# Two late units take their whole first stage in the seven-product form, and the hand-written plans of units 4 to 8 are reordered

## The chip, the core and the metric

The kernel runs on one core of one Trainium2 chip. The metric is the device time of one execution, in microseconds (us). TensorE (PE in the profile; its weight loads are PEld), VectorE (DVE), ScalarE (ACT), GpSimd (POOL) and SyncE (SP, which issues DMAs) each work through a queue of their own, in order, and wait for each other by semaphores.

## The reference

Pooled attention is followed by an MLP mixer over tokens and channels. Eight batches, eight heads, 576 tokens, head width 64:

```
k_p, v_p = mean of 8 neighbouring tokens of k, v          # 72 keys
attn     = softmax(q @ k_p.T / sqrt(64));  x = attn @ v_p # x: 576 x 512 per batch, heads side by side
h  = relu(x.T @ w_tok1) @ w_tok2                           # 576 -> 256 -> 576, over tokens
u  = x + h.T
out = u + relu(u @ w_ch1) @ w_ch2                          # 512 -> 1536 -> 512, over channels
```

All in float32 at the interface; the kernel works in bf16 with float32 sums.

## The kernel before, in words

The channel MLP is the bulk of the work, and it is cut into nine *units* of 512 rows: units 0 to 7 are 512 tokens of batches 0 to 7, and unit 8 gathers the 64 left-over tokens of all eight. A unit has two stages. The first makes `GT = relu(w_ch1.T @ uT)`, 12 tiles of 128 channels by 512 rows (each tile is four matmuls of 512 columns, `l1_tiles`, L561, and an ACT relu, L564). The second multiplies GT by `w_ch2` and adds u.

From unit 2 on the second stage (`unit_fast`) is done in a form of Strassen's that needs seven block products instead of eight; its `product` (L777) is 12 matmuls of 256 columns. It needs four sums of blocks of GT (`g_sums`, written `=1` to `=4` in the plans, VectorE, L614 and L625, kept in the tile `area`) and adds its results with `plus` (L799).

From unit 3 on a part of the first stage has the same form (`first_fast`). The 12 tiles fall into three groups g: tiles 2g, 2g+1, 6+2g, 7+2g. `GROUPS` says which groups of a unit are done by seven products of four 256-column matmuls (L695); the others are plain tiles. One such group takes three ACT copies of sums (L733, L739, L747), three VectorE joins (`joined`, L704) with relus (L707), and one ACT relu (L723). It needs

- sums of the weights, made once per group: `in_weight_sum(i, g)`, written `%ig` in the plans; i below 4 is a VectorE operation (L664), 4 to 6 an ACT copy (L660);
- sums of blocks of uT, made per unit: `token_sum`, written `^ib` (VectorE, L614).

The last two of the seven products of a group are called `seventh` and `fourth`. Both add to the buffer of px: seventh accumulates, a VectorE join reads it, fourth accumulates on, and an ACT relu reads it. For all but the last group they are issued during the next group. For the last group they stand between the plain tiles that come last.

The rest of the work (attention, token MLP) belongs to the batch one or two ahead and is woven into the units. A unit is a generator that yields after every few matmuls, and `PLANS[n]` is a list written out by hand: at yield number i, the named steps are issued. A bare name is a step of batch n+1, `>` of n+2, `<` of n. Names that matter here: `V0 V1 K0 K1` pool v and k (POOL, L277); `kpT` PE transposes of pooled k (L283, L285); `Q0 Q1` transposes of q (DVE, L345); `s0 s1 s2` scores and exponentials (PE L357, ACT L362); `av0..av4` attention times v (PE L391, DVE L395 and L396); `at0 at1` the token MLP's first half (PE L453, ACT L446); `u0..u4` its second half (PE L468, DVE L470); `r0..r3` transposes of u to uT by PE with an ACT copy (L480, L481), `t4` the same for the tails. For batches 6 and 7 uT goes over DRAM instead: `M0 M2` write u out (`mem`, SP, L488), `M` loads it back (`v`, SP, L494) and `T0..T3` finish it (DVE, L499). `+k2c`, `+v3c` issue POOL DMAs that add the next rows of k or v to those already in (L145); POOL waits in its queue for the DMA before.

A plan sets the order on each engine's queue, not a time. Matmul results lie in two pools: `ps_one` with four buffers, taken in turn, and `ps_two` with two buffers of twice the size. A product that takes a buffer waits until what read it last is done.

Of the kernel before, what the change touches and what calls it, by code (L numbers as in the profile page):

```python
# [14 lines left out]
SUMMED = 4  # L15
BOUNCED = 6
FAST = 2
GROUPS = {3: (1,), 4: (1,), 5: (1,), 6: (1,), 7: (1, 2), 8: (1, 2)}
EARLY = 3
POOLE = mybir.EngineType.Pool  # L20
DVE = mybir.EngineType.DVE
# [36 lines left out]
}  # L58


# [1 line left out]
def kernel(  # L62
# [14 lines left out]
    nc = tc.nc  # L77
    B, H, S, D = q.shape
    P = 128
# [29 lines left out]
    w_ch2 = singles.tile([P, NM, DM], BF16)  # L109
    GT = singles.tile([P, NM, 4 * P], BF16)  # L110
# [494 lines left out]
    NH = NM // 2  # L605
    fast = {}
    lo, hi = slice(0, 256), slice(256, 512)
# [71 lines left out]
    def first_fast(n, u):  # L679
        x, U = u["uT"], token_sums(n)  # L680
        gs = GROUPS[n]
        if len(gs) == 1:
            C = [keep(name) for name in ("s1", "s5", "s4")]
            C.insert(1, C[1])
        else:
            if "C" not in fast:
                slots = att.tile([P, H * S + BP], BF16, name="ex")[:, 0:4096].bitcast(FP32).rearrange(
                    "p (i c n) -> p i c n", i=4, c=2)
                fast["C"] = [slots[:, i] for i in range(4)]
            C = fast["C"]  # L690

        def product(ps, w, mv, start=True, stop=True):
            for i in range(2):
                for k in range(2):
                    nc.tensor.matmul(out=ps[:, i], lhsT=w(i, k), rhs=mv(k), start=start and (i, k) == (0, 0),  # L695
                                     stop=stop and k == 1, skip_group_check=True)

        def bank(name):
            if name == "x":
                return ps_two.tile([P, 2, 512], FP32, name="p2")[:, 0].rearrange("p (i n) -> p i n", i=2)  # L700
            return ps_one.tile([P, 2, 256], FP32, name="p1")

        def joined(ps, other, dst):
            nc.vector.tensor_tensor(out=dst, in0=ps, in1=other, op=ALU.add)  # L704

        def relu(part):
            nc.vector.tensor_scalar_max(out=part, in0=part, scalar1=0.0)  # L707

        def summed(i, g):
            if i < 4 or (i, g) in fast.get("at", {}):  # L710
                return lambda r, k: in_sums(i, g)[:, k, r]
            m, k0 = ((2 * g, 0), (2 * g, 2), (NH + 2 * g, 2))[i - 4]
            return lambda r, k: w_ch1[(m + r) // 4][:, k0 + k, (m + r) % 4:512:4]

        def seventh(g, ps):
            sec = pairs_of(g)[1]
            product(ps, summed(2, g), lambda k: U[:, 2, k], start=False)
            joined(ps, C[1 + g % 2], GT[:, sec, hi])
            relu(GT[:, sec, hi])

        def fourth(g, ps):
            product(ps, summed(6, g), lambda k: U[:, 3, k], start=False)
            nc.scalar.activation(out=GT[:, pairs_of(g)[1], lo], in_=ps, func=AF.Relu)  # L723

        plain = [2 * g + r for g in range(3) if g not in gs for r in range(2)]
        for m in plain:
            yield from l1_tiles(u, [m])
        before = None
        for g in gs:
            f, sec = pairs_of(g)  # L730
            px, pz, py = bank("x"), bank("z"), bank("y")
            product(px, summed(4, g), lambda k: x[:, k, lo])
            nc.scalar.copy(out=C[0], in_=px)  # L733
            yield
            if before is not None:
                seventh(g - 1, before)
                yield
            product(pz, summed(0, g), lambda k: U[:, 0, k])
            nc.scalar.copy(out=C[1 + g % 2], in_=pz)  # L739
            yield  # L740
            product(py, summed(5, g), lambda k: x[:, 2 + k, lo])
            joined(py, C[0], GT[:, f, lo])
            if g == gs[-1]:
                relu(GT[:, f, lo])
            yield
            product(px, summed(1, g), lambda k: U[:, 1, k], start=False)
            nc.scalar.copy(out=C[3], in_=px)  # L747
            yield
            product(pz, summed(3, g), lambda k: x[:, 2 + k, hi], start=False)
            joined(pz, C[3], GT[:, f, hi])  # L750
            relu(GT[:, f, hi] if g == gs[-1] else GT[:, f])
            yield
            if before is not None:
                fourth(g - 1, before)
                yield
            before = px
        g = gs[-1]
        tiles = (step for m in plain for step in l1_tiles(u, [NH + m]))
        for i, _ in enumerate(tiles):
            yield  # L760
            if i == 0:
                seventh(g, before)
                yield
            elif i == 2:
                fourth(g, before)
                yield
        if not plain:
            return lambda: seventh(g, before), lambda: fourth(g, before)

    def unit_fast(n, u):  # L770
        last = n == B
        late_steps = yield from (first_fast if n in GROUPS else first_stage)(n, u)

        def product(ps, a, w, start, after, split=False):
            for i in range(2):
                for m in range(NH):
                    nc.tensor.matmul(out=ps[i] if split else ps[:, i], lhsT=a(m)[:, i * P:(i + 1) * P], rhs=w(m),  # L777
                                     start=start and m == 0 and (i == 0 or split), stop=(m == NH - 1),
                                     skip_group_check=True)
                    if (i * NH + m) % 4 == 3 and (i, m) != (1, NH - 1):  # L780
                        yield
                if split:
                    after(i)
            if not split:
                after(slice(0, 2))
            yield

        def bank(split=False):
            if split:
                return [ps_two.tile([P, 2, 512], FP32, name="p2")[:, 0, 0:256] for _ in range(2)]  # L790
            return ps_one.tile([P, 2, 256], FP32, name="p1")

        def plus(out, ps, other, then=None):
            def go(i):
                src, dst = ps[i] if type(ps) is list else ps[:, i], out[:, i]
                if len(other.shape) == 4:
                    src, dst = (x.rearrange("p (a r) -> p a r", a=4) if type(i) is int else
                                x.rearrange("p c (a r) -> p c a r", a=4) for x in (src, dst))
                nc.vector.tensor_tensor(out=dst, in0=src, in1=other[:, i], op=ALU.add)  # L799
                if then is not None:  # L800
                    then(i)
            return go
# [22 lines left out]
        s1 = keep("s1")  # L825
        for i, _ in enumerate(product(x, lambda m: GT[:, m, lo], lambda m: w_ch2[:, m, lo], True,
                                      plus(s1, x, u1lo), last)):
            yield
            if late_steps and i < 2:
                late_steps[i]()  # L830
                yield
        yield from product(y, lambda m: GT[:, NH + m, lo], lambda m: w_ch2[:, NH + m, lo], True, plus(oa[:, :, lo], y, s1))
        z = bank()
        s5 = keep("s5")
        yield from product(z, lambda m: SG[:, 0, m], lambda m: TW[:, 0, m], True, plus(s5, z, u2hi))
# [132 lines left out]
```

## Time and profile before

| | |
|---|---|
| median of 3 runs | 271.18 us (270.85 to 271.25) |
| the profiled execution | 271.6 us |
| its span, first to last instruction | 269.8 us |
| granted TensorE clock | 1.00 |
| first matmul of units 4, 5, 6, 7, 8 | 145.97, 174.84, 205.15, 226.44, 245.42 us |

The first unit begins after the early loads; units overlap with the attention of the batches ahead until unit 6, and units 7 and 8 stand nearly alone. In the timeline, one row can be several equal instructions (x20); the length of such a row runs from the first's start to the last's end. In rows of matmuls the end is modelled, so the price of one is taken from the distance between starts. Some matmul records are missing.

### The profile page before, as it was taken

How to read it: one execution, taken by the hardware profiler on the slowest of the kernel's cores; microseconds unless marked ns; L12 is line 12 of the kernel's file. 1: busy time of each engine (PE TensorE's matmuls, PEld its weight loads, DVE VectorE, ACT ScalarE, POOL GpSimd, SP SyncE). 2: the span in 40 equal slices, each digit the busy share in tenths (PEclk: the TensorE clock that was granted, in tenths of full speed). 3: DMA queues.
4: the chain of work that ended last, by engine and by line, in shares of the span. 5: the costliest groups of instructions: out<-in, count | busy, mean ns of one | idle time of the engine just before them, and what ended most of it. 6: DMA issues, size and time to landing. Idle time of an engine off the chain costs nothing.

```text
span 269.8 us, 5432 instructions
## 1 busy us (share of the span) xinstructions
PE 259.5 (96%) x2173; PEld 171.7 (64%) x2200; DVE 206.8 (77%) x427; ACT 122.7 (45%) x207; POOL 113.4 (42%) x114
## 2 busy tenths in 40 slices
PE   8999999999999999999999999999999999999992
PEld 2776454545544645776587657864785688787781
DVE  4755573751798859996978798899799889997981
ACT  1375773047444353736563637264922632613600
POOL 5847749999995428636657242420000000000000
PEclk9999999999999999999999999999999999999999
DMA  7999999959969898998995997361506510404106
GB/s 184 190 194 205 204 212 204 180 126 190 153 132 140 154 159 118 146 169 168 155 141 83 156 213 87 39 164 40 119 0 147 149 18 21 137 2 116 41 2 157
DMA packets 42081, 35.17 MB, mean 130 GB/s; under 512 B 12040, under 2 KB 34408, under 8 KB 42056
## 3 DMA queue, kind: packets, MB, share of 16 engines
q0 software_dynamic: 30672, 22.11, 55.3%
q1 hardware_dynamic: 11056, 12.39, 17.2%
q10 hardware_dynamic: 328, 0.33, 0.5%
q8 instruction: 17, 0.28, 0.4%
q14 instruction: 8, 0.07, 0.1%
HBM read 36.90 MB, written 10.49 MB: 176 GB/s over the span
## 4 chain that ended last, share of the span: by engine, by line
PE 90%; DVE 5%; ACT 2%; issue 1%; DVEq 0%
PE p L777 24%; PE p L561 22%; PE p L695 9%; PE p L592 8%; PE p L453 6%; PE p L468 5%; PE p L357 4%; PE p L391 3%; PE p L862 3%; PE p L480 2%; PE p L323 1%; DVE area L614 1%; DVE u L470 1%; ACT ex L379 1%; ACT x L426 1%
## 5 line engine op out<-in xcount | busy, mean ns | idle before, releaser
L564 ACT ACTIVATE GT<-p 128x512 bf16<-128x512 f32 x76 | 44.5, 596 | 57.6 <-PE p L561 43.7
L561 PE MATMUL p<-uT,w_ch 128*128 128x512 bf16 x274 | 69.3, 380 | 0.9 <-issue 0.4
L561 PEld LDWEIGHTS <-w_ch 128*128 128x128 bf16 x304 | 32.4, 114 | 24.1 <-issue 1.7
L362 ACT ACTIVATE ex<-p 72x1024 bf16<-72x1024 f32 (+1 forms) x42 | 31.6, 804 | 27.5 <-PE p L357 27.3
L777 PEld LDWEIGHTS <-area 128*128 128x128 bf16 x336 | 31.9, 98 | 5.3 <-issue 1.3
L777 PE MATMUL p<-area,area 128*128 128x256 bf16 x252 | 30.8, 273 | 0.0
L145 POOL DMA_DIRECT2D kr<-in_k_dram x16 | 23.4, 1495 | 15.6 <-DMA kr<-in_k_dram 15.6
L145 POOL DMA_DIRECT2D vr<-in_v_dram x16 | 23.1, 1478 | 14.2 <-DMA vr<-in_v_dram 14.2
L470 DVE TENSOR_TENSOR u<-p,x 128x512 bf16<-128x512 f32 x32 | 21.1, 680 | 8.2 <-PE p L468 8.2
L777 PEld LDWEIGHTS <-GT 128*128 128x128 bf16 x252 | 24.2, 98 | 4.9 <-issue 0.6
L592 PE MATMUL p<-w_ch,GT 128*128 128x512 bf16 x92 | 23.6, 379 | 0.2
L777 PE MATMUL p<-w_ch,GT 128*128 128x256 bf16 x168 | 20.6, 273 | 0.1
L799 DVE TENSOR_TENSOR o<-p,s 128x512 f32<-128x512 f32 (+1 forms) x28 | 17.9, 662 | 3.2 <-PE p L777 3.1
L396 DVE TENSOR_TENSOR x<-p,den 128x512 bf16<-128x512 f32 x28 | 19.4, 691 | 1.0
L468 PE MATMUL p<-AT,w_tok 128*128 128x512 bf16 x62 | 17.3, 379 | 0.5 <-DVE u L470 0.5
L799 DVE TENSOR_TENSOR s<-p,u 128x512 f32<-128x512 f32 x24 | 16.2, 680 | 2.0 <-PE p L777 2.0
L395 DVE RECIPROCAL den<-p 128x8 f32<-128x8 f32 (+1 forms) x35 | 7.0, 201 | 11.3 <-PE p L391 10.9
L391 PEld LDWEIGHTS <-ex 72*128 72x128 bf16 x280 | 12.6, 98 | 3.9 <-DVE x L396 0.2
L592 PEld LDWEIGHTS <-GT 128*128 128x128 bf16 x96 | 8.8, 98 | 9.4 <-issue 0.4
L453 PE MATMUL p<-x,w_tok 128*128 128x512 bf16 x53 | 13.7, 379 | 0.2
L446 ACT ACTIVATE AT<-p 128x512 bf16<-128x512 f32 x14 | 8.4, 597 | 12.1 <-PE p L453 11.7
L391 PE MATMUL p<-vp,ex 72*128 72x65 bf16 x280 | 13.7, 194 | 0.0
(151 smaller groups left out, 448.8 us busy)
## 6 DMA issues: line engine op xcount, KB each, us to landing
out_dram<-o SPq DMA_DIRECT2D x34, 256.0 KB, 3.8
kr<-in_k_dram POOLq DMA_DIRECT2D x16, 288.0 KB, 7.4
vr<-in_v_dram POOLq DMA_DIRECT2D x16, 288.0 KB, 7.0
qb<-in_q_dram POOLq DMA_DIRECT2D x7, 576.0 KB, 10.1
kr<-in_k_dram POOLq DMA_DIRECT2D x3, 576.0 KB, 10.9
vr<-in_v_dram POOLq DMA_DIRECT2D x3, 576.0 KB, 12.4
w_ch<-in_moe_w_ch_dram POOLq DMA_DIRECT2D x6, 256.0 KB, 10.6
w_ch<-in_moe_w_ch_dram POOLq DMA_DIRECT2D x3, 512.0 KB, 13.1
```

The lines of the kernel that those rows point to most:

```text
L145: nc.gpsimd.dma_start(out=pair_sums(b, key), in_=src[:, :, 2 * i * D:2 * (i + 1) * D], accum_op=ALU.add if i else ALU.bypass)
L362: nc.scalar.activation(out=exv[:, a, :, gs[0]:gs[-1] + 1, n0:n0 + n], func=AF.Exp, scale=scale, in_=pss[a][0:SP, :, 0:len(gs) * n].rearran ...
L391: nc.tensor.matmul(out=ps[:, h // 4, (h % 4) * (D + 1):(h % 4 + 1) * (D + 1)], lhsT=st["ex"][:, h * S + n0:h * S + n0 + P], rhs=st["vp"][: ...
L453: nc.tensor.matmul(out=ps, lhsT=w_tok1[:, c if c < 4 else 4 + par, m * P:(m + 1) * P], rhs=st["x"][:, c, :] if c < 4 else st["xt"], start= ...
L468: nc.tensor.matmul(out=ps, lhsT=w, rhs=a, start=(i == 0), stop=(i == len(mms) - 1))
L470: nc.vector.tensor_tensor(out=quads_of(dst, on), in0=plain_of(ps, on), in1=plain_of(x, on), op=ALU.add)
L561: nc.tensor.matmul(out=ps[m], lhsT=w_ch1[m // 4][:, kk, m % 4:512:4], rhs=moving(u)[kk], start=(kk == 0), stop=(kk == 3))
L564: nc.scalar.activation(out=GT[:, m, :], in_=ps[m], func=AF.Relu)
L592: nc.tensor.matmul(out=ps, lhsT=GT[:, m, c * P:(c + 1) * P], rhs=w_ch2[:, m, :], start=(m == 0), stop=(m == NM - 1))
L695: nc.tensor.matmul(out=ps[:, i], lhsT=w(i, k), rhs=mv(k), start=start and (i, k) == (0, 0), stop=stop and k == 1, skip_group_check=True)
L777: nc.tensor.matmul(out=ps[i] if split else ps[:, i], lhsT=a(m)[:, i * P:(i + 1) * P], rhs=w(m), start=start and m == 0 and (i == 0 or spli ...
L799: nc.vector.tensor_tensor(out=dst, in0=src, in1=other[:, i], op=ALU.add)
```

## The change

- `GROUPS` of units 7 and 8 becomes (0, 1, 2): no plain tiles are left in their first stage. Sums of group 0's weights (`%00` to `%60`) are added to the plans of units 4 and 5.
- With no plain tiles, `first_fast` hands seventh and fourth of the last group back (`late_steps`). `unit_fast` issues seventh after the first four matmuls of the first block product x and fourth after x's last; product y then takes the first four of its six channel tiles for both halves before the last two (`late`), since the last two are what fourth writes. (The old code had this path, with other places, but no unit used it.)
- The px of groups 0 and 1 take `ps_two` buffers where there are three groups, that of group 2 a `ps_one` buffer.
- The plans come in a new order. Those of units 2 and 3 come out the same; the first difference is at step 18 of unit 4. Among the moves: r3, r0 and r1 of unit 4 come earlier; five VectorE weight sums stand between unit 4's last yield and unit 5's `u3 u2 u0 u1` (`%00 %10 %22 %20 %30`), and two that stood there (`%02 %12`) now stand behind; four of the u of batch 7 with their `M2 M0` go from unit 6 to the end of unit 5; three of the four token sums of unit 7 go to unit 6.

```diff
-GROUPS = {3: (1,), 4: (1,), 5: (1,), 6: (1,), 7: (1, 2), 8: (1, 2)}
+GROUPS = {3: (1,), 4: (1,), 5: (1,), 6: (1,), 7: (0, 1, 2), 8: (0, 1, 2)}
...
     4: {0: "^04 ^14", 2: "^34", 3: "av4 av0", 5: ">K1", 9: "av3 >K0", 11: ">Q0 at0 at1", 12: "u4", 13: ">kpT",
-        15: "u2 u3", 16: "+v2c", 17: "r2 >Q1", 18: "u1 u0 >s1", 19: "=1a t4 +k3a", 20: "=3b", 22: "=1b =2a +v3a",
-        26: "lq3", 27: "r0 =2b =4a =3a >V1", 28: ">s0 =4b", 31: "+k3b", 34: ">V0 >av0 r1 >av1", 37: "r3",
-        39: ">av2 +v3b", 40: ">av3"},
-    5: {0: "%61", 1: "+k2c >K1 s2", 2: ">Q0 ^05", 6: "^25", 7: "^15 av4", 8: ">Q1", 9: ">K0 +v2c >kpT ^35 %22",
-        11: "%02", 13: "%12 at0 at1", 15: "u3 u2 M2 u1", 16: "u0 =3a", 18: ">s1 =1a", 20: "M0 M",
-        22: ">V1 =2a =4a >V0 =1b =2b", 24: "%62 =4b >s0", 29: ">av2 >av0", 32: ">av3", 33: "%41 >av1", 35: "%52",
-        37: "=3b >s2", 39: ">av4 %51", 40: "T3 T1 T0 >at0", 41: "T2 >at1", 43: ">u4"},
-    6: {1: "u3", 2: "u2 u1 M2 u0", 4: "^06", 7: "^16 ^36 ^26 M0", 9: "%32", 15: "M", 16: "t4", 18: "=1a =2a",
-        22: "%42 =1b", 23: "=3b =4a", 24: "=3a", 27: "=2b =4b", 35: "T0 T2", 36: "T3 T1", 39: "^07"},
-    7: {1: "^17 ^37", 7: "^27", 17: "=12 =22", 20: "=11 =21 =41", 22: "^08 =10 =20", 26: "=30", 28: "^28", 31: "=40",
-        33: "=31", 34: "=42", 36: "=32", 37: "^18", 42: "^38"},
-    8: {3: "=30", 18: "=32 =11 =12 =22", 20: "=31", 21: "=10", 24: "=21", 26: "=20 =40 =42", 30: "=41"},
+        15: "u2 u3", 16: "+v2c", 17: "r2 >Q1", 18: "u1 r3 u0 >s1", 19: "=1a t4 +k3a", 20: "=3b",
+        22: "r0 r1 =1b =2a +v3a", 26: "lq3", 27: "=2b =4a =3a >V1", 28: ">s0 =4b", 31: "+k3b", 33: "^25",
+        34: ">V0 +v3b +v3c >av0 >av1", 39: ">av2", 40: ">av3", 41: "%40 %60", 43: "%00 %10"},
+    5: {1: "^05 ^15", 3: "%22 %20", 5: ">Q0 s2 +k2c", 7: ">V1", 8: "av4", 12: "=3b >Q1 at0 at1 ^35", 13: "%30",
+        15: "u3 u2 u0 u1", 16: "%41", 18: ">K0 >K1 >kpT", 20: ">s1", 21: "%02 %12 =1a =2a =4a =3a", 22: "=1b >V0",
+        24: ">s0 =2b", 25: "=4b M2 %62", 29: ">av2 >av0", 30: "M0", 33: ">av3 >av1", 34: "%52", 36: "M", 37: ">s2",
+        39: ">av4 %51 %42", 40: "T3 T2 >at0 %50 >at1 T1", 41: ">u2", 42: "T0 >u3 >u1 >M2 >u0 >M0"},
+    6: {3: "%32", 4: "^06", 6: "M", 9: "^26 ^16 ^36", 12: "u4", 16: "t4 =3b", 20: "=3a =1a =2a", 21: "=4a",
+        23: "^28", 24: "=1b", 27: "=2b =4b", 30: "T2", 31: "T1", 33: "T3", 36: "T0", 37: "^27 ^07", 41: "^17"},
+    7: {2: "^37", 20: "=11 =12 =10", 21: "=21", 23: "=20", 25: "=22", 26: "=30 =42", 27: "=41", 28: "=40", 29: "^08",
+        32: "=32", 33: "=31", 40: "^18 ^38"},
+    8: {6: "=30", 9: "=10", 22: "=12", 24: "=20 =11 =22", 25: "=21", 27: "=40", 30: "=41 =42", 31: "=31", 33: "=32"},
...
         def bank(name):
-            if name == "x":
+            if name == "x" and len(gs) < 3 or name in ("x0", "x1"):
...
-            px, pz, py = bank("x"), bank("z"), bank("y")
+            px, pz, py = bank(f"x{g}" if len(gs) == 3 else "x"), bank("z"), bank("y")
...
-        def product(ps, a, w, start, after, split=False):
-            for i in range(2):
-                for m in range(NH):
+        def product(ps, a, w, start, after, split=False, late=False):
+            parts = [range(4), range(4, NH)] if late else [range(NH)]
+            for j, (i, m) in enumerate((i, m) for part in parts for i in range(2) for m in part):
...
-            if late_steps and i < 2:
-                late_steps[i]()
+            if late_steps and i in (0, 2):
+                late_steps[i // 2]()
                 yield
-        yield from product(y, lambda m: GT[:, NH + m, lo], lambda m: w_ch2[:, NH + m, lo], True, plus(oa[:, :, lo], y, s1))
+        yield from product(y, lambda m: GT[:, NH + m, lo], lambda m: w_ch2[:, NH + m, lo], True, plus(oa[:, :, lo], y, s1),
+                           late=bool(late_steps))
```

More of the change, by code (lines that the diff above doesn't have):

```diff
@@ L772, in unit_fast @@
         late_steps = yield from (first_fast if n in GROUPS else first_stage)(n, u)
-        def product(ps, a, w, start, after, split=False):
-            for i in range(2):
-                for m in range(NH):
[L777 to L782, printed above, removed]
+        def product(ps, a, w, start, after, split=False, late=False):
+            parts = [range(4), range(4, NH)] if late else [range(NH)]
+            for j, (i, m) in enumerate((i, m) for part in parts for i in range(2) for m in part):
+                nc.tensor.matmul(out=ps[i] if split else ps[:, i], lhsT=a(m)[:, i * P:(i + 1) * P], rhs=w(m),
+                                 start=start and m == 0 and (i == 0 or split), stop=(m == NH - 1),
+                                 skip_group_check=True)
+                if j % 4 == 3 and (i, m) != (1, NH - 1):
+                    yield
+                if split and m == NH - 1:
                     after(i)
```

## The prediction

> **What bounds the kernel now.** I read the page's first part, then busy time by stretches, then the chain that ended last, then the timeline of the stretches that the change touches. The page and the stretches (columns: stretch, length, then busy time and instructions of PE, PEld, DVE, ACT, POOL, the clock, DMA share, GB/s):
>
> ```profile
> PE 259.5 (96%) x2173; PEld 171.7 (64%) x2200; DVE 206.8 (77%) x427; ACT 122.7 (45%) x207; POOL 113.4 (42%) x114
> ...
> 176.00:214.00 38.00, 37.84 (x322) 24.86 (x314) 35.02 (x70) 20.22 (x35) 1.60 (x2) 1.00 0.37 98
> ...
> 233.00:252.00 19.00, 18.89 (x157) 15.54 (x157) 16.55 (x37) 6.86 (x13) 0.00 (x0) 1.00 0.20 56
> ```
>
> TensorE sets the time at a granted clock of 1.00, but VectorE is busy for 35.02 of 38 us around unit 5 and 16.55 of 19 in unit 7: whatever is given to it there has little room. The chain of waits (start, length, what) shows a late unit:
>
> ```profile
> 208.33 2.16 PE p L561 x10
> ...
> 226.87 1.46 PE p L561 x6
> 228.33 5.37 PE p L695 x48
> 233.96 0.60 PE p L695 x4
> 234.56 0.86 PE p L561 x4
> 235.43 0.56 PE p L695 x4
> 236.41 9.17 PE p L777 x84
> ```
>
> A 512-column matmul (L561) takes 2.16/10 = 0.216 us of TensorE's time and a 256-column one (L777) 9.17/84 = 0.109. A product of four half matmuls is 0.437. First stages start at 145.97 (unit 4), 174.84 (5), 205.15 (6), 226.44 (7) and 245.42 (8); the last matmul ends at about 264.6. From the counts of matmuls and these prices, units 4 to 8 hold 28.2, 29.6, 21.1, 18.7 and 18.7 us of matmuls in 28.9, 30.3, 21.3, 19.0 and 19.2: only 2 us of idle in all. So matmuls taken out shorten the kernel, and each new wait lengthens it.
>
> **Matmuls out, in units 7 and 8.** Each loses 16 matmuls of 512 columns (tiles 0, 1, 6, 7) and gains 7 products: 16 x 0.216 = 3.46 against 28 x 0.109 = 3.06. Twice 0.40 is **-0.80**. Bounds: a first stage's first 20 half matmuls, from 228.17 to 230.48, took 2.31, or 0.1155 each; at that price the two units save 2 x 0.22 = 0.44. No row is cheaper than 0.109, so the ends are -0.80 and -0.44. I take 0.109, which 84 in a row show.
>
> The Trainium skill ("TensorE: Matmul & The Clock Gate", section Back-to-back issue gap) speaks against this edit: it gives a sustained spacing of some 81 ns at 128 columns and 131 ns at 512. By it, with 98 ns at 256 as an estimate of mine between the two, 28 x 98 ns is more than 16 x 131 ns, and each unit would lose 0.65 us instead of gaining. The trace disagrees: 216 and 109 ns, in proportion to the columns.
>
> **The moved products (late steps).** In the old order seventh and fourth stand between plain tiles, 0.86 apart; TensorE waited 235.39 - (234.40 + 4 x 0.216) = 0.13 for the join that reads the bank in between (0.19 in unit 8). Now eight half matmuls of x, 0.87, stand between them: the same wait. Fourth's ACT eviction (0.60 and some 0.26 around it) has the eight matmuls of y's first part, 0.87, as cover. **0**; without that cover 0.86 per unit, since y reads what fourth writes. VectorE gets three more joins and their relus per unit, 3 x (0.72 + 0.21) = 2.8, and loses three token sums (1.0) to the unit before: 16.55 + 1.8 = 18.35 of some 18.6. I followed its order join by join: each is done before the product that needs its bank, by 0.1 to 0.8 us. Cover is thin; bounds 0 to +1.1 (a rival).
>
> **The input weight sums of group 0.** Four VectorE sums (L664, 0.60 apart) and three ACT copies (L660, 0.66), now in units 4 and 5. Unit 5's timeline (start, length, engine, line):
>
> ```profile
> 177.24 1.40 DVE L614 TENSOR_TENSOR t<-uT 128x512 bf16<-128x512 bf16 x2
> ...
> 181.19 0.68 DVE L664 TENSOR_TENSOR kr<-w_ch,w_ch 128x512 bf16<-128x512 bf16 x1
> ...
> 181.79 0.68 DVE L704 TENSOR_TENSOR GT<-p,s 128x512 bf16<-128x512 f32 x1
> ...
> 182.51 0.29 DVE L707 TENSOR_SCALAR GT<-GT 128x512 bf16<-128x512 bf16 x1
> ...
> 185.78 2.48 DVE L470 TENSOR_TENSOR u<-p,x 128x512 bf16<-128x512 f32 x4
> ...
> 187.91 1.01 PE L357 MATMUL p<-qD,kD 32*72 32x512 bf16 x8
> ```
>
> An independent operation starts 0.60 after a 0.68 one, a dependent relu 0.72 after. In the new order VectorE has, from the end of unit 4's outputs (176.57) to the first u of batch 6: five weight sums (two of them were there later), 5 x 0.60 + 0.12; three token sums, 1.12; two q transposes, 1.38; memsets 0.08; av4's two, 0.84; three joins with relus, 2.79; =3b, moved ahead, 0.57; the add itself, 0.68. Sum 10.6, so u3 is out at 187.15. TensorE issues the four u and then the next plain tile, which takes u3's buffer of the four in ps_one: by the same prices it arrives 11.6 after 174.84, at 186.4. **+0.75** of waiting in which the queue behind it, fourth, kpT and scores, stands. Bounds: 0.2 if every pair overlaps as independent ones do; 1.4 if POOL's pooling falls into it: the first row above has two sums in 1.40 where the others take 0.41, beside POOL's vp of 176.75. By the order POOL now finishes V1, K and V0 of batch 7 before that, so I leave it out.
>
> **Scores of unit 5.** In the last row a score group took 1.01 where the others take 0.65: its second bank waited for fourth's eviction. Now a tile and the kpT stand ahead, fourth is older: **-0.35** (bounds -0.36 and 0).
>
> **Unit 4, transposes r3, r0, r1 moved ahead.** The same 12 PE transposes, but ACT copies and buffers come earlier:
>
> ```profile
> 161.40 1.93 ACT L362 ACTIVATE ex<-p 72x1024 bf16<-72x1024 f32 x2 [0.78 <-PE p L357]
> ...
> 163.22 1.07 ACT L564 ACTIVATE GT<-p 128x512 bf16<-128x512 f32 x2
> 163.27 2.35 PE L777 MATMUL p<-w_ch,GT 128*128 128x256 bf16 x20
> ```
>
> With r0 and r1 between, the first block product takes the buffer of the first of those two relus, which stands behind both exponentials. These begin 0.22 later (r3), so the relu ends at about 164.1; TensorE, 0.67 us of transposes later than 163.27, is there at 163.95: **+0.20** (0 to 0.5).
>
> **The u of batch 7 from unit 6 to the end of unit 5.** Eight matmuls go and come: 0. Between at1 and u2's second matmul lie 0.65 us, while at1's relu needs 0.85, and copy %50 stands in ACT's queue ahead of it: **+0.25** (0.1 to 0.5). On SP the spills M2 and M0 now go ahead of unit 5's second pair of stores; the loads M have a first stage, some 11 us, until the transposes T, and mem and v landed in 3: 0. POOL's +v3c and +k2c swap places; kpT needs their pooling at 188, some 10 us later than it can be done: 0. Small bank waits of unit 5's second stage: **+0.10** (0 to 0.3).
>
> Sum: -0.80 + 0.75 - 0.35 + 0.20 + 0.25 + 0.10 = **+0.15**. The profiled execution took 271.6 (span 269.8 and 1.8 around it), 0.4 above the median 271.18; the difference carries over: **271.3 us**. A measurement of this kernel tells about 0.2% (0.54 us) from no change, so this is "no change": 270.64 to 271.72.
>
> **Rivals.** *The unit 5 wait is small.* Speaking for it: 0.57 of VectorE's sum is dependence gaps, and TensorE may itself be late. With 0.2 there and ACT's relus in time (0.1 instead of 0.25), the sum is -0.80 + 0.20 - 0.35 + 0.20 + 0.10 = -0.65: **270.5**. Against it: VectorE was already 0.4 late for u3 (185.78 against 185.15 + 0.2). 0.25.
>
> *VectorE becomes the bound of units 7 and 8.* Its 18.35 against 18.6 leaves 0.25 of idle per unit; in 233 to 252 it now idles 2.45. From the point where it must wait for products for more than 0.25 us, the rest is paid by TensorE. Half of today's idle, 1.2, would cost 0.95 in unit 7; unit 8 has no token sums, no cost. With 0.15 that is **272.3**, slower. For it: the row 233 to 252; against it: much of the idle lies where group 2's outputs end and can be filled by moved sums. 0.28.
>
> *The half products don't save what they should*, at 0.1155 each: -0.44, **271.7**, at the edge of slower. For it, the first products of each first stage; against it, 84 in 9.17. 0.05.
>
> The forecast has 0.42. Faster 0.25, within 0.2% 0.42, slower 0.28 + 0.05 = 0.33. The forecast alone spans 270.6 to 271.8; for 8 in 10 the range reaches to the first rival's lower side and the second's value: 270.3 to 272.4.
>
> **What would show it.** Unit 7's and 8's first stages without L561, and each unit from first L695 to the next at about 18.6; a gap of about 0.75 before an L561 near 186.6 with a DVE L470 as its releaser; no 1.01 score group; an ACT wait of some 0.2 before the first L777 of unit 4. Wrong: TensorE waits for joins (L704) all through units 7 and 8, or unit 5 shows no wait for L470.

## The result and the profile after

The changed kernel is slower: 273.03 us median (271.40 to 277.14, 18 runs) against 271.20 for the kernel before (270.03 to 273.30, 18 runs), ratio 1.0062, interval 1.0045 to 1.0078. Of 271.2 us that is 1.68 us, interval 1.22 to 2.12. Some executions run at a lower granted clock and take some 2% longer; medians count them, ratios leave them out. The forecast was 271.3, no change, in a range of 270.3 to 272.4; the median lies 0.6 above the upper end. The profiled execution took 272.72 us with a span of 271.0.

The page's busy times, and busy time in units 5, 7 and 8, each from its first matmul to the next unit's first (columns: stretch, length, then busy time and instructions of PE, PEld, DVE, ACT, POOL, the clock, DMA share, GB/s), of the kernel after, then the same units before:

```profile
PE 258.9 (96%) x2200; PEld 173.4 (64%) x2224; DVE 212.5 (78%) x441; ACT 123.7 (46%) x209; POOL 113.9 (42%) x114
```

```profile
174.53:207.62 33.09, 31.10 (x276) 20.34 (x279) 31.67 (x61) 17.41 (x30) 3.25 (x3) 1.00 0.31 81
...
227.97:246.39 18.42, 18.42 (x171) 16.40 (x169) 18.07 (x41) 6.86 (x12) 0.00 (x0) 1.00 0.21 58
246.39:265.50 19.11, 18.87 (x170) 16.03 (x167) 18.01 (x42) 6.87 (x12) 0.00 (x0) 1.00 0.23 62
```

```profile
174.84:205.15 30.31, 30.15 (x276) 19.97 (x277) 28.28 (x57) 16.33 (x28) 1.60 (x2) 1.00 0.35 85
...
226.44:245.42 18.98, 18.88 (x156) 15.45 (x157) 17.80 (x40) 6.78 (x12) 0.00 (x0) 1.00 0.20 57
245.42:264.60 19.18, 19.04 (x156) 15.36 (x156) 15.74 (x36) 6.78 (x12) 0.00 (x0) 1.00 0.23 63
```

TensorE has less to do and VectorE 5.7 us more (212.5 against 206.8). The clock is 1.00 in every stretch. Of these 33.09 us of unit 5 VectorE is busy for 31.67, of unit 7's 18.42 for 18.07.

The table gives the lengths of units 4 to 8 in all profiles, cut in the same way, with one correction. In after, e2, e3, e4 and e9 the record of unit 5's first matmul is missing. The distance from its first row to the next scores shows it (timeline of after, then of e7):

```profile
174.53 2.54 PE L561 MATMUL p<-uT,w_ch 128*128 128x512 bf16 x11
177.00 0.33 PE L357 MATMUL p<-qD,kD 32*72 32x64 bf16 x16
```

```profile
174.30 2.75 PE L561 MATMUL p<-uT,w_ch 128*128 128x512 bf16 x12
176.99 0.33 PE L357 MATMUL p<-qD,kD 32*72 32x64 bf16 x16
```

Eleven records and 2.47 us stand against twelve and 2.69 in e7, so the unit began one matmul, 0.216 us, ahead of its first record. The table counts that matmul to unit 5 and takes it from unit 4: unit 5 of after is 33.30 long, not 33.09. "VectorE" is its busy time in units 5, 7 and 8, "u3" the time for which TensorE stands before the tile that takes u3's buffer in unit 5. In the three rows with "(6)" a net 0.87 us of the u of batch 7 stands in unit 6, in the others in unit 5, so units 5 and 6 are read together.

| kernel | unit 4 | 5 | 6 | 7 | 8 | 5+6 | VectorE 5 / 7 / 8 | u3 |
|---|---|---|---|---|---|---|---|---|
| before (6) | 28.87 | 30.31 | 21.29 | 18.98 | 19.17 | 51.60 | 28.28 / 17.80 / 15.74 | 0 |
| after | 28.75 | 33.30 | 20.35 | 18.42 | 19.08 | 53.65 | 31.88 / 18.07 / 18.01 | 1.24 |
| e1 (6) | 28.97 | 31.63 | 21.79 | 19.48 | 19.07 | 53.42 | | 0 (0.31 at a u's bank) |
| e2 | 28.91 | 31.15 | 20.35 | 18.98 | 19.16 | 51.50 | | 0 |
| e3 | 29.13 | 32.25 | 20.60 | 18.42 | 19.07 | 52.84 | | 0 |
| e4 | 28.75 | 32.36 | 20.34 | 18.43 | 19.07 | 52.71 | | 1.20 |
| e5 | 29.15 | 31.90 | 20.34 | 18.46 | 18.79 | 52.24 | 30.49 / 17.51 / 17.64 | 0.74 |
| e6 | 28.76 | 31.15 | 20.35 | 18.42 | 19.08 | 51.50 | | 0 |
| e7 | 28.88 | 31.15 | 20.35 | 18.42 | 19.08 | 51.50 | 28.41 / 18.07 / 18.02 | 0 |
| e8 | 28.76 | 31.15 | 20.34 | 18.46 | 18.79 | 51.49 | 27.87 / 17.51 / 17.64 | 0 |
| e9 | 28.75 | 31.15 | 20.35 | 18.46 | 18.79 | 51.50 | 28.39 / – / 17.64 | 0 |
| e10 (6) | 28.83 | 31.17 | 21.30 | 18.99 | 19.17 | 52.47 | 28.51 / – / – | 0.93 (at a u's bank) |

From before to after, units 4 to 8 grow by -0.12 + 2.05 - 0.56 - 0.09 = 1.28 us, which lies in the interval of the ratio. (Unit 4 began 0.41 us earlier in the profiled execution of after; the plans up to there are the same in both.) The loss is all in unit 5. In the new order that unit takes 31.15 wherever TensorE doesn't wait for VectorE in it (e2, e6 to e9), and the other rows with this order are longer by their waits.

The chain of waits of the kernel after, in unit 5 (start, length, what):

```profile
168.46 6.35 DMA kr<-in_k_dram
174.80 1.27 DVE o L799 x2
176.07 0.95 DVE kr L664
...
177.05 1.22 DVE kr L664
...
187.29 0.61 DVE u L470
...
187.94 0.59 PE p L561 x2
```

Before, the chain was TensorE's through the late units (90% of the span by the page's fourth part). After, it leaves TensorE for VectorE for 13 us. (The DMA's row ends where the next piece of the chain begins, not where it landed; POOL, which waits for it, goes on at 175.62. VectorE shows no idle time ahead of its two outputs, and nothing below rests on that link.) Here is what the chain's rows stand beside, from the timeline (start, length, engine, line):

```profile
175.62 2.10 POOL L277 TENSOR_TENSOR kp<-kr 72x256 bf16<-72x256 f32 x2 [1.59 <-DMA kr<-in_k_dram]
175.99 1.02 DVE L664 TENSOR_TENSOR kr<-w_ch 128x512 bf16<-128x512 bf16 x1
177.05 1.22 DVE L664 TENSOR_TENSOR kr<-kr,w_ch 128x512 bf16<-128x512 bf16 x1
177.69 1.18 POOL L277 TENSOR_TENSOR vp<-vr 72x256 bf16<-72x256 f32 x1
178.25 0.90 DVE L614 TENSOR_TENSOR t<-uT 128x512 bf16<-128x512 bf16 x1
...
179.20 0.60 PE L695 MATMUL p<-t,t 128*128 128x256 bf16 x4 [0.18 <-DVE t L614]
...
182.38 0.38 PE L453 MATMUL p<-xt,w_tok 128*128 128x512 bf16 x1 [0.40 <-DVE xt L396]
...
187.94 0.59 PE L561 MATMUL p<-uT,w_ch 128*128 128x512 bf16 x2 [1.09 <-DVE u L470]
```

POOL pools batch 7's last keys and values exactly when VectorE does `%00`, `%10` and a token sum. They take 1.02, 1.22 and 0.90 us, where the same operations take 0.68, 0.69 and 0.38 in e5: VectorE is 1.4 us late, and TensorE waits three times for it: for the token sum, for xt, and for the add of u3. By the price of a matmul the last gap is 187.94 - (184.97 + 8 x 0.216) = 1.24 us. Counted from starts in the same way, the first two are 0.35 and 0.57. Together that is 2.16, and 31.15 + 2.16 = 33.31.

### The profile page after: what moved, and what is told of

It reads as the page before. It is cut to its first block, busy times and chain, and to the rows that moved or that the text cites. A ratio compares the mean times of both kernels' runs of the same rounds, so it can differ in the third digit from the quotient of the medians.

```text
span 271.0 us, 5504 instructions
## 1 busy us (share of the span) xinstructions
PE 258.9 (96%) x2200; PEld 173.4 (64%) x2224; DVE 212.5 (78%) x441; ACT 123.7 (46%) x209; POOL 113.9 (42%) x114
## 4 chain that ended last, share of the span: by engine, by line
PE 51%; DMA 29%; DVE 7%; POOL 5%; issue 4%; ACT 2%; POOLq 0%
DMA kr<-in_k_dram 15%; DMA vr<-in_v_dram 14%; PE p L777 13%; PE p L561 11%; PE p L695 7%; PE p L592 5%; PE p L863 3%; PE p L468 3%; PE p L453 2%; DVE GT L704 2%; PE p L357 2%; PE p L391 1%; POOL kp L277 1%; PE p L323 1%; DVE kr L664 1%
## 5 line engine op out<-in xcount | busy, mean ns | idle before, releaser
L561 PE MATMUL p<-uT,w_ch 128*128 128x512 bf16 x262 | 65.5, 380 | 2.0 <-DVE u L470 1.1
L564 ACT ACTIVATE GT<-p 128x512 bf16<-128x512 f32 x68 | 39.9, 597 | 41.4 <-PE p L561 30.3
L561 PEld LDWEIGHTS <-w_ch 128*128 128x128 bf16 x272 | 28.8, 114 | 23.5 <-issue 3.1
L470 DVE TENSOR_TENSOR u<-p,x 128x512 bf16<-128x512 f32 x32 | 21.2, 681 | 9.3 <-PE p L468 9.3
L396 DVE TENSOR_TENSOR x<-p,den 128x512 bf16<-128x512 f32 x28 | 19.4, 691 | 1.0
L799 DVE TENSOR_TENSOR o<-p,s 128x512 f32<-128x512 f32 (+1 forms) x28 | 18.0, 662 | 1.6 <-PE p L777 1.6
L799 DVE TENSOR_TENSOR s<-p,u 128x512 f32<-128x512 f32 x24 | 16.2, 680 | 1.8 <-PE p L777 1.7
L277 POOL TENSOR_TENSOR vp<-vr 72x256 bf16<-72x256 f32 x8 | 9.5, 1194 | 9.6 <-DMA vr<-in_v_dram 6.7
```

The costliest lines, as they stand in the source:

```text
L396: nc.vector.tensor_tensor(out=dst.rearrange("p (a h d) -> p a h d", a=2, d=D), in0=view[:, :, :, 0:D], in1=den[rows, :, :, None].broadcast ...
L470: nc.vector.tensor_tensor(out=quads_of(dst, on), in0=plain_of(ps, on), in1=plain_of(x, on), op=ALU.add)
L561: nc.tensor.matmul(out=ps[m], lhsT=w_ch1[m // 4][:, kk, m % 4:512:4], rhs=moving(u)[kk], start=(kk == 0), stop=(kk == 3))
L564: nc.scalar.activation(out=GT[:, m, :], in_=ps[m], func=AF.Relu)
```

## Experiments

Four theories of the loss. **Q**: VectorE's queue in front of the u's of unit 5 is too long (the weight sums of the third group and POOL's collision with them). **G**: the third seven-product group does not pay where it stands, in units 7 and 8. **O**: the new order of the plans costs by itself. **P**: POOL's collision alone costs, not the sums. Each kernel was timed against the kernel before.

### e1: the third group without the new order

```diff
 after's GROUPS and plans of units 7 and 8; before's plans of units 4 to 6, and in them
+4: {41: "%40 %60", 43: "%00 %10"}, 5: {26: "%20", 30: "%50"}, 6: {11: "%30", 25: "^28", 39: "^27 ^07", 41: "^17"}
-5: {0: "%61"}
```

> The new GROUPS, late steps and plans of units 7 and 8, but the plans of units 4 to 6 of the kernel before, with the seven sums of group 0 put at unit 4's end (four), in unit 5's second stage (two) and in unit 6 (one), and three token sums in unit 6. Theory Q (the loss is VectorE's queue in unit 5's first stage; units 7 and 8 do gain): two VectorE sums instead of five ahead of the u of batch 6, two POOL poolings there instead of three; TensorE waits under 0.4 us before the plain tile that takes u3's buffer (1.24 in the changed kernel); units 7 and 8 together 0.6 us shorter than before (18.42 and 19.11 against 18.98 and 19.18), total 0.5 us below the kernel before, ratio 0.998. Rival G (the third seven-product group does not pay): ratio 1.002 or more, with the loss in units 7 and 8.

Measured 273.57 us against 271.3, ratio 1.0089 (1.0055 to 1.0123). Unit 5 is at 31.63, unit 6 0.50 longer than before, and unit 7, which should gain, is 0.50 longer than before. This misses the 0.998 that Q gave, and by its number alone it would speak for G; the waits say otherwise. TensorE of e1 waits in unit 6 for a join and in unit 7 for a token sum:

```profile
216.22 0.60 PE L695 MATMUL p<-t,w_ch 128*128 128x256 bf16 x4 [0.35 <-DVE GT L704]
...
229.15 0.61 PE L695 MATMUL p<-qb,kr 128*128 128x256 bf16 x4 [0.50 <-DVE qb L614]
```

VectorE as the bound of unit 7, a rival of the prediction, is real if its sums are not moved. The places of the moved sums in this kernel are mine, so it tells of one such placement only.

### e2: the new order without the third group

```diff
-7: (0, 1, 2), 8: (0, 1, 2)}
+7: (1, 2), 8: (1, 2)}
 after's plans of units 4 to 6 without %00 to %60; before's plans of units 7 and 8 without ^17 ^27 ^28
```

> The old GROUPS and unit 7 and 8 plans (token sums that now stand in unit 6 taken out), none of group 0's seven sums, but the new order in units 4 to 6. Theory Q: four of the five weight sums ahead of the u are gone (2.5 us of VectorE), so the 1.24 us wait goes to 0 or 0.2 although POOL's poolings still fall there; unit 5 is 1.7 us shorter than in the changed kernel, total 0.0 to 0.5 above the kernel before, ratio 1.000 to 1.002. Rival O (the order alone, whatever the sums): ratio 1.006 or more. Rival P (POOL's collision alone makes the wait): a wait of 0.8 or more stays before the plain tile, ratio 1.004.

Measured 271.41 against 271.3, ratio 1.0011 (0.9991 to 1.0031). No TensorE wait for VectorE in unit 5, and units 5 and 6 together are 0.10 shorter than before. O falls. P isn't tested here: in e2's profile POOL pools batch 7's k at 177.36, beside a transpose of VectorE and not a sum.

### e3: three sums moved behind the u's

```diff
-5: {3: "%22 %20", 13: "%30"}
+5: {27: "%22", 31: "%20"}, 6: {10: "%30"}
```

> The changed kernel with three of the five VectorE weight sums (%22, %20, %30) taken from ahead of the u of batch 6 and put into unit 5's second stage (two) and unit 6 (one). Theory Q: VectorE reaches u3 1.8 us earlier, the wait of 1.24 us and the 0.36 us one of at0 for xt go to 0 to 0.2; unit 5 from 33.1 to 31.7, total 1.3 us below the changed kernel, ratio to the kernel before 1.001. Rival P (POOL's collision alone): the waits stay at 0.8 or more, ratio 1.005.

Measured 272.31, ratio 1.0032 (1.0015 to 1.0050). The u's come in time, as Q says. P would say so too, since in this profile POOL was done with batch 7 at 176.34, ahead of VectorE's first sum at 176.84: there was no collision. But units 5 and 6 are still 1.24 longer than before. The new wait is in the second stage of unit 5 of e3, where `%22` and `%20` (L664 at 194.29 and 197.77, 0.68 each) now stand in front of attention's normalizations (timeline of e3):

```profile
197.31 0.43 PE L391 MATMUL p<-vp,ex 72*128 72x65 bf16 x8 [0.17 <-DVE x L396]
...
200.19 0.32 PE L357 MATMUL p<-qD,kD 32*72 32x64 bf16 x14 [0.55 <-DVE x L396]
```

Unit 5 has no room for these sums in either stage.

### e4: POOL's order as before

```diff
-4: {34: "... +v3b +v3c ..."}, 5: {5: "... +k2c", 7: ">V1", 18: ">K0 >K1 ...", 22: "... >V0"}
+4: {39: "... +v3b"}, 5: {1: "+k2c >K1 ...", 9: ">K0 +v2c", 22: "... >V1 >V0"}
```

> The changed kernel with POOL's queue in the old order (batch 7's k finished and pooled before the last rows of v are fetched), all else as changed. Theory Q: one POOL pooling pair instead of three operations falls on VectorE's first operations of unit 5, which took 1.4 us longer than they do alone; about 0.7 of that comes back, the wait of 1.24 falls to 0.5, total 0.7 to 1.0 below the changed kernel, ratio to the kernel before 1.003. Rival P (POOL's collision alone): the wait goes to 0 to 0.2, ratio 1.000. If POOL has no part: ratio stays 1.006.

Measured 272.11, ratio 1.0024 (1.0003 to 1.0045). The two small waits are gone and unit 5 is 0.94 shorter, but the wait at u3's tile is still 1.20. In the timeline of e4 the early sums are quick, and POOL's other pair hits `=3b`, which takes 0.56 where it stands alone:

```profile
175.34 0.68 DVE L664 TENSOR_TENSOR kr<-w_ch 128x512 bf16<-128x512 bf16 x1
176.05 0.69 DVE L664 TENSOR_TENSOR kr<-kr,w_ch 128x512 bf16<-128x512 bf16 x1
...
182.14 1.03 DVE L614 TENSOR_TENSOR area<-GT 128x768 bf16<-128x768 bf16 x1
```

So P as told of the early pair does not explain it: with that collision gone, over half of the loss in units 5 and 6 remains (52.71 against 51.60; after has 53.65). What stands in front of the u's is still five sums, and a collision of 0.5 in another place.

### e5: two relus of each of units 7 and 8 on ScalarE

```diff
+        due = []
...
             joined(ps, C[1 + g % 2], GT[:, sec, hi])
-            relu(GT[:, sec, hi])
+            due.append(GT[:, sec, hi]) if len(gs) == 3 and g < 2 else relu(GT[:, sec, hi])
...
-            nc.scalar.activation(out=GT[:, pairs_of(g)[1], lo], in_=ps, func=AF.Relu)
+            nc.scalar.activation(out=GT[:, pairs_of(g)[1], lo], in_=ps, func=AF.Relu); flush()
+        flush = lambda: [nc.scalar.activation(out=p, in_=p, func=AF.Relu) for p in due] and due.clear()
...
-            nc.scalar.copy(out=C[1 + g % 2], in_=pz)
+            nc.scalar.copy(out=C[1 + g % 2], in_=pz); flush()
```

> The changed kernel with one difference: in units 7 and 8 the relu of the seventh products' half of the hidden layer (L707, groups 0 and 1) goes from VectorE (0.29 us each) to ScalarE, which is idle for 11 us of each of these units. If VectorE's full queue is what keeps unit 8 at 19.1 us (it has no idle time from 246 to 263, and the last seventh product's bank is joined 0.38 late), unit 8 loses 0.2 to 0.4 us, unit 7 at most 0.1, and the ratio falls from 1.006 to about 1.005. If unit 8 is set by its matmuls and the third group does not pay there for another reason, its 19.1 stays. Unit 5 stays at 33.1 by every theory.

Measured 272.30 against 271.1, ratio 1.0042 (1.0013 to 1.0072). Unit 8 is 0.29 shorter, as expected of a full VectorE, and the wait for the last seventh's bank is gone. The row of after that has no counterpart in e5:

```profile
256.87 0.60 PE L695 MATMUL p<-qb,vr 128*128 128x256 bf16 x4 [0.21 <-DVE GT L704]
```

Unit 5 was expected at 33.1 "by every theory", and it is 31.90: a miss, and the most useful row of the series. In this profiled execution the granted clock was 0.90 in the first 50 us (1.00 in after), so unit 5 began 4.0 us later than in after, while batch 7's rows had landed as early as ever. POOL's pair was done before VectorE came to its sums. Timeline of e5:

```profile
174.98 1.64 POOL L277 TENSOR_TENSOR kp<-kr 72x256 bf16<-72x256 f32 x2 [1.83 <-DMA kr<-in_k_dram]
...
180.00 0.68 DVE L664 TENSOR_TENSOR kr<-w_ch 128x512 bf16<-128x512 bf16 x1
180.71 0.69 DVE L664 TENSOR_TENSOR kr<-kr,w_ch 128x512 bf16<-128x512 bf16 x1
...
190.54 0.59 PE L561 MATMUL p<-uT,w_ch 128*128 128x512 bf16 x2 [0.58 <-DVE u L470]
```

Without the collision the gap before u3's tile is 190.54 - (188.07 + 8 x 0.216) = 0.74 us. VectorE needs 190.48 - 180.08 = 10.40 us from unit 4's outputs to the end of the add, and 187.89 - 176.07 = 11.82 in after, with the collision. One profile is not the whole run: units 4 to 8 of this one add up to what before has (118.64 and 118.62 us), while e5's ratio stands for 1.1 us more than before (0.4 to 2.0). So its other executions lost time that this one's units don't show; a collision in most of them would fit, but none of them was profiled.

### e6, e7: the weight sums where VectorE idles

```diff
-4: {43: "%00 %10"}, 5: {3: "%22 %20", 13: "%30"}
+3: {10: "%00 %10 ..."}, 4: {11: ">Q0 %30 ...", 20: "%20 %22 =3b"}
```

Two slots of their own (2 KB per partition) hold `%00` and `%10`, and the old kr tile is taken over before the vr tile, as soon as batch 6's keys are pooled. e6 has POOL's old order as well (as in e4), e7 the new one.

> The changed kernel with the five input weight sums of VectorE (%00 %10 %20 %30 %22) taken out of the last steps of unit 4 and of unit 5's first stage and put where VectorE idles: %00 and %10 in unit 3 at step 10 (into two slots of their own), %30 in unit 4 at step 11, %20 and %22 in unit 4 at step 20; and batch 7's pooling on POOL in the order of the kernel before. If VectorE's queue ahead of the u's is what costs, the waits at the tile that takes u3's buffer, at xt and at the token sum are gone, unit 5 is 30.9 to 31.2 us, units 6 to 8 keep 20.35, 18.4 and 19.1, unit 4 gains at most 0.2, and the ratio to the kernel before is 0.998 to 1.000. If POOL's collision alone costs, it does no better than the old POOL order alone: unit 5 near 32.1, ratio 1.002. If the third group does not pay, 1.002 or more.

> As the run before, but with the changed kernel's own order of batch 7's pooling on POOL. With VectorE's queue as the cause, the sums being gone leaves slack enough that a collision of 1.4 us at most shows in part: unit 5 30.9 to 31.6 us, ratio 0.999 to 1.002. With the collision as the cause, unit 5 stays at 32.1 or more wherever POOL's pairs fall on VectorE's first ops of unit 5, ratio 1.003 or more.

Measured, both against 271.1: e6 271.33, ratio 0.9997 (0.9972 to 1.0022); e7 270.95, ratio 0.9972 (0.9942 to 1.0002). In both, unit 5 is 31.15 with no wait for VectorE in the first stage, and units 5 and 6 together are 0.10 shorter than before. Moving five sums of 0.6 us, none removed, takes back the whole loss of these units. The collision was there in e7's profile too: its second token sum took 0.95 instead of 0.43. G falls with them: e7 differs from e2 in the third group and its sums, and where the sums stand free, units 7 and 8 are 0.64 us shorter than in e2 (18.42 and 19.08 against 18.98 and 19.16).

### e8, e9: early sums and relus together, with the old and the new POOL order

> The early sums with the old POOL order, and the relus of units 7 and 8 on ScalarE as well. If both waits are VectorE's queue, they add up: unit 5 about 31.0, unit 8 18.7 to 18.9, ratio 0.996 to 0.999, faster than both kernels. If unit 8 is set by its matmuls, it equals the run without the relus moved.

> Early sums and relus on ScalarE, with the changed kernel's own POOL order. If VectorE's slack in unit 5 now absorbs POOL's collision, it equals the same kernel with the old POOL order within 0.2%: unit 5 31.15, unit 8 18.8, ratio 0.995 to 0.999. If the collision still costs, unit 5 is 31.5 to 32 and the ratio 1.000 or more.

Measured: e8 270.79 against 271.1, ratio 0.9975 (0.9953 to 0.9996); e9, in a later series, 271.06 against 271.4, ratio 0.9987 (0.9966 to 1.0008). e9 decides between Q and P, for in its profile the collision is there and the sums are not (timeline, then unit 5 by the stretch):

```profile
175.88 2.11 POOL L277 TENSOR_TENSOR kp<-kr 72x256 bf16<-72x256 f32 x2 [1.64 <-DMA kr<-in_k_dram]
```

```profile
176.34 0.95 DVE L614 TENSOR_TENSOR t<-uT,t 128x512 bf16<-128x512 bf16 x1
...
178.92 0.20 DVE L395 RECIPROCAL den<-p 64x8 f32<-64x8 f32 x1 [0.94 <-PE p L391]
```

```profile
174.41:205.34 30.93, 30.62 (x276) 20.30 (x279) 28.17 (x56) 17.40 (x30) 2.80 (x3) 1.00 0.36 88
```

The token sum takes 0.95 instead of 0.43, but VectorE then still idles 0.94 before its next operation, and the unit is 31.15 long with its missing first matmul. The four cases together: late sums with the collision 33.30 (after), late sums without it 31.90 (e5), early sums with it 31.15 (e7, e9) and without it 31.15 (e8; in e6 one relu late in the stage took 0.51 instead of 0.29). The sums cost 0.75 us where they stand. POOL's work at the start of the unit costs another 1.4 beside the sums and nothing without them. That nothing has two parts: with the sums gone VectorE loses only 0.5 us there, since fewer of its operations are of the kind that POOL holds up, and its idle time covers that.

### e10: the kernel before with such a relu on ScalarE

```diff
 before, and the edit of e5 for group 1
```

> The kernel before with one difference: the relu of the seventh product's half of group 1 in units 7 and 8 on ScalarE. It tells whether the gain of the early sums with the relus moved comes from the third group or would be had without it. VectorE has 1.2 us (unit 7) and 3.4 us (unit 8) idle there before, so nothing waits for it: units 7 and 8 keep 18.98 and 19.17 within 0.1, ratio 0.998 to 1.002. If the relus alone make the gain, 0.997 or less.

Measured 271.9 against 271.4, ratio 1.0006 (0.9985 to 1.0027); units 7 and 8 at 18.99 and 19.17. So what e8 gains does not come from the relus alone. Its profile shows something else: unit 5, whose code is that of before, is 31.17 where before's profile has 30.31. There v landed late, and POOL's pair met a sum and a relu of VectorE in front of the u's (1.21 and 0.63 us instead of 0.67 and 0.29):

```profile
182.67 1.46 POOL L277 TENSOR_TENSOR vp<-vr 72x256 bf16<-72x256 f32 x2 [6.74 <-DMA vr<-in_v_dram]
```

```profile
187.78 0.59 PE L468 MATMUL p<-AT,w_tok 128*128 128x512 bf16 x2 [0.77 <-DVE u L470]
```

The gap is 187.78 - (186.42 + 2 x 0.216) = 0.93 us: the kernel before pays for the collision too, in executions in which the rows land so.

## Why the prediction was wrong

**The step that failed** is the bound of the wait at u3's buffer: "1.4 if POOL's pooling falls into it", then "By the order POOL now finishes V1, K and V0 of batch 7 before that, so I leave it out." The collision was put at nothing by the order of POOL's list alone. POOL comes early in its list, but it waits for its rows: in after it stands idle until the DMA of kr has landed, and its three additions run from 175.62 to 178.87, over the very sums that the change put there. In the old order k's last rows were fetched ahead of v's and pooled at 169.37; in the new order they come last. Nor does the order settle it: in the six profiles with the new order k is pooled 3.3 us before (e5), 1.2 before (e3), and 1.0 (e7), 1.3 (after), 1.7 (e9) and 3.0 us after (e2) unit 5's first matmul.

**The wait without it was sized well.** Predicted: VectorE 10.6 us from unit 4's outputs to the add, TensorE at the tile after 11.6, wait 0.75. Measured in e5: 10.40, 11.48 and 0.74. Over units 5 and 6 the terms 0.75 - 0.35 + 0.25 + 0.10 made 0.75; e5 has 0.64, after 2.05. The missing 1.3 us is the collision (1.41 between e5 and after). It went beyond its bound too: 1.4 was to be the whole wait, and TensorE waited 2.16 in all. The 1.24 at u3's tile lies within it; the waits for the token sum and for xt had no term.

**The matmuls out**: -0.80 predicted, -0.65 measured. Unit 7 gains 0.56: its 0.40, and the wait of 0.13 for the late join, which the prediction kept, is gone. (The three token sums that leave unit 7 are two of its own, `^17` and `^27`, and `^28` of unit 8; `^07` stood in unit 6 before.) The price of a half matmul holds: 76 of them take 8.31 us in the chain of after, 0.109 each, and no L561 is left there:

```profile
216.80 2.16 PE p L561 x10
218.96 9.17 PE p L777 x84
228.13 8.31 PE p L695 x76
```

Unit 8 gains only 0.09. That "unit 8 has no token sums, no cost" was wrong: two of its own token sums and the last outputs of unit 7 run over into it (L614 at 246.23, L799 at 247.03), two g_sums (`=30`, `=10`) stand between its joins, VectorE goes from 15.74 to 18.01 of 19.1 us, and the last seventh comes 0.38 late. With two relus less on VectorE, e8's unit 8 gains 0.38 against before and units 7 and 8 together 0.90. The forecast's 18.6 per unit came out as 18.42 and 19.08.

**The smaller terms.** Unit 4 came out 0.12 shorter, not 0.20 longer: the first block product does wait 0.14, but a wait of 0.31 for a u in front of the transposes at 159.09, which before's profile has, is gone. The 1.01 score group is gone as predicted, its row has 0.65; the next score group, in the second stage, takes 0.86 where it took 0.65 before, so of the 0.35 some 0.1 is left. u2's wait for at1's relu is about 0.20 (0.25).

**The rivals.** VectorE did become the bound, which was the slower rival, but in unit 5 and a little in unit 8, not in unit 7, where the new order prevents it (e1 shows it without that). The half products cost what 0.109 says; the rival at 0.1155 falls. The first rival, a small wait in unit 5, is what e6 to e9 reach by another road. That the measured 1.68 is above the 1.28 of the profiled units is not explained: it lies within the interval, and each execution has its own landing times; how often the collision falls on the sums in unprofiled runs was not measured.

## What to carry to other kernels

Where an engine is busy for over 90% of a stretch, cost added work by the place where it stands in that engine's queue, and look for idle time in earlier stages: five sums of 0.6 us cost 0.75 us (2.15 with a collision) ahead of a buffer that TensorE waits for, and nothing one or two units earlier. A bound that depends on two engines not meeting must be checked against what releases the second one; if that is a DMA, its landing is the time, not its place in a list, and the bound belongs into the likely value. What stands in the queue decides what a collision costs: POOL's additions at the same place cost 1.4 us in one order and nothing in another. And look at how many matmuls a row counts before its gap is called a wait: here a missing record looked like 0.2 us.

## What the runs showed of the hardware

POOL's and VectorE's additions slow each other when both read SBUF. POOL's kp pair went from 1.64 to 2.10 us and its vp from 0.72 to 1.18, while VectorE's L664 went from 0.68 to 1.02 and 1.22. VectorE's operations that read one operand from PSUM are not touched. In the profile of after between 60 and 200 us, seven normalizations (L396), six u adds (L470) and five joins and outputs (L600, L704, L799) lie beside POOL's additions for over 60% of their time and take 0.65 to 0.69 us as ever. Of the bf16 operations with SBUF operands alone that lie so, six of eight are longer: L664 as told, three sums of L614 (0.90, 1.52 and 0.85 instead of 0.38, 0.42 and 0.55) and a relu, L707 (0.67 instead of 0.29).

How long such an operation gets can be read from the ends of the rows. In after POOL's kp pair ends at 177.72, the second L664 0.55 later, POOL's vp 0.60 after that, and the token sum 0.28 after POOL. The same remainder comes back in e1 and e10, where L664 ends 0.55 and 0.54 after POOL's pair (timeline of e1, then of e10, whose pair of 182.67 is shown above):

```profile
176.00 1.86 POOL L277 TENSOR_TENSOR vp<-vr 72x256 bf16<-72x256 f32 x2 [4.37 <-PE p L357]
...
177.31 1.10 DVE L664 TENSOR_TENSOR kr<-kr,w_ch 128x512 bf16<-128x512 bf16 x1
```

```profile
183.46 1.21 DVE L664 TENSOR_TENSOR kr<-w_ch 128x512 bf16<-128x512 bf16 x1
```

So the two engines took turns here: the end of one's operation plus a fixed remainder is the end of the other's. The two that kept their time (0.55 at 100.82, 0.54 at 105.35) had an addition of POOL beside them that took 1.25 and 1.94, so there POOL was the late one.

The Trainium skill ("SBUF — State Buffer", section Who interferes with whom) says so: an operation of VectorE with two SBUF inputs, or one in a two-port mode such as a tensor_scalar may take, contends with a GpSimd instruction that reads SBUF, and one with at most one SBUF input outside those modes does not. The trace agrees: those with a PSUM operand keep their time, and the slowed ones have two SBUF inputs or are a tensor_scalar (the relu). The page also says that the later one blocks until the first is finished. The rows fit that: both sides grow (by 1.4 us on VectorE and 0.9 on POOL in after), in turns, with the same remainder behind each wait.
